# Clearing of the third V tile moved behind the first pair's row maxima; the first q and the first three weight units loaded through ScalarE's queue

## The chip, the cores and the metric

The kernel runs on one core of one Trainium2 chip. The metric is the device time of one execution in microseconds, the median of three runs. TensorE (PE) does the matrix products, VectorE (DVE), ScalarE (ACT) and GpSimd (POOL) the rest; SyncE (SP) computes nothing and starts transfers between the chip's main memory and its on-chip memory. Every engine works through its own list of instructions in order, and waits where an instruction needs a result that is not there.

## What is computed

```python
def reference(q, k, v, w_gate, w_val, w_out, w2_in, w2_out):
    # q, k, v: (2 batches, 12 heads, 448 tokens, 64), float32; weights float64
    scores = q @ k.transpose(0, 1, 3, 2) / 8
    scores = where(strictly_upper_triangle, -1e9, scores)
    attn = exp(scores - max(scores)); attn = attn / (sum(attn) + 1e-9)
    x = (attn @ v), heads side by side            # (896, 768)
    x = (sigmoid(x @ w_gate) * (x @ w_val)) @ w_out            # inner width 1536
    h = x @ w2_in                                              # inner width 2048
    return (h * clip(h + 3, 0, 6) / 6) @ w2_out                # (896, 768)
```

## The kernel before, in words

A float32 operand is carried to TensorE as two parts, `hi` and `lo = x - hi`, and each product is three matmuls (hi·hi, hi·lo, lo·hi). ACT writes the `hi` parts, DVE the `lo` parts.

**Attention** works on 12 pairs of heads. All work of a pair is cut into steps, each bound to an engine. A list scheduler (`emit_in_order`) goes through them with estimated durations and writes the instructions out in the order in which they would start by these estimates; this order is fixed when the kernel runs. In the texts a step has the pair's number in brackets:

- `Lk`, `Lq`, `Lv` (SP): load k, q, v of the pair, two transfers each (`load`, lines 208 to 227).
- `Tk`, `Tq` (PE, L247): transposes, all through one PSUM buffer `tr`, which the next transposition takes over only after `Tlk` or `Tlq`. `Thk`, `Thq` (ACT, L256): hi parts `kh`, `qh`. `Tlk`, `Tlq` (DVE, L263): lo parts `kl`, `ql`.
- `S0`, `S1`, `S2` (PE, L279 and L289): scores of query tiles 0 and 1, of tile 2, and of tile 3, with the mask added. There are two PSUM buffers for them.
- `M0` to `M3` (DVE, L300, `s_max`): row maxima of the four query tiles. `E0` to `E3` (ACT, L307, L311): exponentials and row sums. `R0` to `R3` (DVE, L316): reciprocals. `N0` to `N3` (POOL, L322): normalisation.
- `C0` to `C3` (PE, L335): transposes of the normalised rows; `H` (ACT, L345) and `J` (DVE, L351) their two parts.
- `Vh`, `Vl` (POOL, L234 and L241): the two parts of V, written into the diagonal blocks of a padded tile `vpad`. There are three such tiles, used in turn (pair p uses tile p mod 3). The off-diagonal blocks must be zero; they are cleared once, at the start, by 12 DVE memsets (L562), four for each tile. Pair 2 is the first to use the third tile.
- `D0` to `D3` (PE, L362): product with V into one buffer `pav`; `Xh` (ACT, L375) and `Xl` (DVE, L378) give it back, and `D0` of the next pair waits for `Xl`.
- 30 steps `Z` (PE, L440): products of zeros that fill the time in which TensorE would stand idle while the first pairs start.

**Weights** come in 68 units of 768 KB of 64-bit words, loaded by `load_unit` (L93, on SP) and decoded by ACT and DVE. The first three units are steps of the schedule: `W0` to `W2` (SP, the load), `Wa` (ACT, L105, scales the upper words), `Wb` (DVE, L110, shifts the lower words), `Wc` to `We` and `Wg` (DVE), `Wf` (ACT). They are decoded among the steps of the pairs, long before TensorE uses them. The order that the scheduler writes out has, on ACT, `E3(2)`, then `Thk(4)`, at the place of `W0`; `H1(2)`, then `E3(3)`, at that of `W1`; and `Wa1`, then `H0(3)`, at that of `W2`. On DVE the order from `Wb0` on is `Wb0`, `R2(3)`, `M3(3)`, `J0(2)`, `Tlq(5)`, `J1(2)`, `Wc0`, `M0(4)`, `M1(4)`, `R3(3)`, `Xl(1)`. On DVE at the start it is the memsets, `Tlk(0)`, `Tlq(0)`, `M0(0)`, `M1(0)`, `M2(0)`, `R0(0)`, `R1(0)`, `Tlq(1)`, `M3(0)`, `R2(0)`, `Tlk(1)`, `R3(0)`, `Tlq(2)`.

**Feed-forward** follows: both layers stream the weight units through TensorE, three units ahead.

Of the kernel before, what the change touches and what calls it, by code (L numbers as in the profile page):

```python
# [8 lines left out]
F32 = mybir.dt.float32  # L9
# [7 lines left out]
PSUM = bass.MemoryType.PSUM  # L17

# A float32 operand is carried to the tensor engine as two float32r parts: hi, rounded to 12
# significant bits, and lo = x - hi, which has at most 12 and so is exact.  A product is  # L20
# hi*hi + hi*lo + lo*hi; lo*lo is below half a unit of the float32 product's last place.
TERMS = ((0, 0), (0, 1), (1, 0))

# float64 weights come as raw 64-bit words.  The upper word read as float32 and scaled by 2**-112
# has the exponent of the float32 value in its low eight exponent bits, three places too far right.
REBIAS = 2.0 ** -112
# The upper word of float32's largest 12-bit value, scaled so: larger magnitudes saturate there.
UPPER_MAX = (1.0 + 0x6FFE00 / 2.0 ** 23) * 2.0 ** (31 - 127)
# [3 lines left out]
def kernel(  # L32
# [12 lines left out]
    nc = tc.nc  # L45
# [5 lines left out]
    CP = 112  # L51
    # Query tiles begin where a chunk of D keys does.
    Q0 = [0, *range(S % P or P, S, P)]
    Q1 = [*Q0[1:], S]
    NQ = len(Q0)
# [15 lines left out]

# [1 line left out]
    units = []  # L73
# [13 lines left out]

    def load_unit(u):
        if u >= NU:
            return  # L90
        src, n = units[u]
        t = wraw.tile([P, UN], U64, tag="raw", name="raw")
        nc.sync.dma_start(  # L93
            out=t.rearrange("p (a b) -> p a b", b=n),
            in_=src.rearrange("(a p) b -> p a b", p=P),
        )
        raw_t[u] = t
# [53 lines left out]
    def acc():  # L151
        """The next of four two-bank accumulators, in turn."""
        pool = psum[acc_n[0] // 2 % 2]
        acc_n[0] += 1
        return pool.tile([P, 2, 512], F32, tag="m", name="m")

    def split(hi, lo, src):
        """src (PSUM or SBUF) into its two parts."""
        nc.scalar.copy(hi, src)
        nc.vector.tensor_sub(lo, src, hi.bitcast(F32))  # L160

    def halves(ps, u, x, k0, first, last, bs=(0, 1), ks=range(6)):
        """ps[f, token] += unit u's [768, 128] block transposed times x, for batches bs."""
        w = split_t[u]
        for i in ks:
            for n, (a, c) in enumerate(TERMS):
                for b in bs:
                    nc.tensor.matmul(  # L168
                        ps[:, b, :S],
                        lhsT=w[a][:, i * P : (i + 1) * P],  # L170
                        rhs=x[c][:, k0 + i, b * S : (b + 1) * S],
                        start=(first and i == 0 and n == 0),
                        stop=(last and i == 5 and n == 2),
                    )
# [6 lines left out]
    with tc.manual_schedule():  # L181
        # ================= attention =================
        with ExitStack() as actx:
# [16 lines left out]
            NV = 3  # L200
            # V by chunks of 64 keys, the first head's over the second's, block diagonal.
            vpad = [
# [5 lines left out]
            def load(p, nm):  # L208
                b, hp = divmod(p, NPAIR)
                if nm == "v":  # L210
                    t = p_raw.tile([P, NC, D], F32, tag=nm, name=nm)
                    for j in range(2):
                        nc.sync.dma_start(
                            out=t[j * D : (j + 1) * D],
                            in_=v[b, 2 * hp + j].rearrange("(c p) d -> p c d", p=D),
                        )
                    live[nm, p] = t
                    return
                t = p_raw.tile([CP, S // CP, 2, D], F32, tag=nm, name=nm)
                for j in range(2):  # L220
                    nc.sync.dma_start(
                        out=t[:, :, j, :],
                        in_=(q if nm == "q" else k)[b, 2 * hp + j].rearrange(
                            "(c p) d -> p c d", p=CP
                        ),
                    )
                live[nm, p] = t

            def halves_of(t):
                return [t[j * D : (j + 1) * D, :, j * D : (j + 1) * D] for j in range(2)]  # L230

            def v_hi(p):
# [36 lines left out]
            def s_pe(p, ts):  # L269
                both = ps_a.tile([P, 2, 512], F32, tag="m", name="s")  # L270
                off = 0
                for t in ts:
# [13 lines left out]
                    for j in range(2):  # L286
                        # Half a tile: in the rows of the array that the head's products use.
                        r = slice(j * D, (j + 1) * D) if rows == D else slice(rows)
                        nc.tensor.matmul(  # L289
                            ps[:, j, Q0[t] :], lhsT=identb[r, r], rhs=maskb[r, r],  # L290
                            start=False, stop=True,
                        )
# [5 lines left out]
            def s_max(p, t):  # L298
                nm = column("nm", t)
                nc.vector.tensor_reduce(nm, live["s", p, t], axis=AX.X, op=ALU.max, negate=True)  # L300
                live["nm", p, t] = nm

            def s_exp(p, t):
# [22 lines left out]
            def c_pe(p, g):  # L326
                ps = ps_pt.tile([P, 512], F32, tag="pt", name="pt")
                for c, off in GROUPS[g]:
                    for t in range(NQ):
                        if Q1[t] > c * D:  # L330
                            # From the middle of a tile: its rows turned by half, and what comes
                            # after the second half is written over or not used.
                            r, rows = max(0, c * D - Q0[t]), Q1[t] - Q0[t]
                            o = off + Q0[t] + r - c * D
                            nc.tensor.transpose(  # L335
                                ps[:, o : o + rows],
                                live["pr", p, t][:, c].rearrange("p j d -> p (j d)"),
                                identf[:rows, r : r + rows],
                            )
# [39 lines left out]

            # Chunks that share a PSUM bank, with their columns there: the longest left, and the  # L380
            # longest that still fits.
            GROUPS, WIDTH, chunks = [], [], list(range(NC))
# [9 lines left out]

            # Query tiles that share a tile of scores, a bank for each head.
            STILES = [(0, 1), (2,), (3,)]

            def product(cols, stationary=P):
                """The weight of a product: its columns, or the load of its stationary operand."""
                return max(cols / 2.4 + 3, stationary / 1.2)

            # Every step of a pair: (key, engine, weight, what it follows, function).  # L400
            steps = []
# [42 lines left out]

            # While the last pairs drain: the first weights, and batch 0's part of their products.
            first_acc = []
            for u in range(3):
# [6 lines left out]

                add("W", "sp", 2000, [], load_unit)
                add("Wa", "act", 740, own("W"), dec_scale)
# [19 lines left out]

            # Buffers: how many, and (step that takes one, step that gives it back) in turn.
            def every(*uses):
# [24 lines left out]
            def emit_in_order(rank):  # L503
                """Emit the steps as a list schedule would start them: of those that can start
                first, the one of least rank."""
                left = {s[0]: s for s in steps}
# [34 lines left out]

            # How far a kind of step falls back, in pairs.
            LATE = {
# [4 lines left out]

            # The tensor engine's clock rises under load: products of zeros keep it busy while the
            # first pairs start.  # L550
            idle = const.tile([P, 512], BF16, name="idle")
# [6 lines left out]
            nc.vector.tensor_copy(maskb, maskf)  # L558
            for pair in vpad:
                for t in pair:  # L560
                    for j in range(2):
                        nc.vector.memset(  # L562
                            t[j * D : (j + 1) * D, :, (1 - j) * D : (2 - j) * D].bitcast(F32), 0.0
                        )
            emit_in_order(rank)
            for u in range(3):
                load_unit(u + 3)

        # ================= feed-forward =================
        LA = 3  # L570
# [73 lines left out]
        for c in range(2):  # L644
# [14 lines left out]
            for s in range(NS - 2):  # L659
# [7 lines left out]
                u += 1  # L667
            # The last two units go by token tile, so that the tiles are done one after another.
            advance(u)
# [43 lines left out]
```

## Time and profile before

| | |
|---|---|
| median of three runs | 624.47 us (624.44 to 624.48) |
| span of the profiled execution, first to last instruction | 620.4 us |
| time of the profiled execution itself | not recorded beside its span; the runs lie 4.07 us above the span |
| TensorE busy | 611.8 us, 99% of the span |
| VectorE, ScalarE, GpSimd busy | 413.4, 267.0, 94.3 us |

The span is what the profile can explain; the 4.07 us around it are launch and end. Busy shares are averages over stages: the attention stage ends at about 130 us, and in it ACT, DVE and POOL are nearly as busy as TensorE, while in the feed-forward stage TensorE alone sets the pace. A matmul's end is modelled, so its start is the better mark.

### The profile page before, as it was taken

The page shows a single profiled execution, that of the slowest core. Times are in us where ns is not written, and L with a number is a line of the kernel's source. Part 1 is how long each engine was busy: PE and PEld are TensorE (multiplying, and loading weights), DVE is VectorE, ACT ScalarE, POOL GpSimd, SP SyncE. Part 2 cuts the span into 40 slices and gives each one's busy share as a digit, 9 for nine tenths or more (in the row PEclk, how much of TensorE's full clock was granted, in tenths as well). Part 3 has the DMA queues.
Part 4 walks back from the last instruction along what each step waited for, and adds up shares of the span by engine and source line. Part 5 has one row for each costly group of instructions (what it writes and reads, how often), then busy time and mean ns, then how long its engine had stood idle before and what let it go on. Part 6 is the DMA issues. An engine that isn't in the chain of part 4 may idle for free.

```text
span 620.4 us, 8945 instructions
## 1 busy us (share of the span) xinstructions
PE 611.8 (99%) x3498; PEld 560.2 (90%) x3498; DVE 413.4 (67%) x604; ACT 267.0 (43%) x532; POOL 94.3 (15%) x152
## 2 busy tenths in 40 slices
PE   8999999999999999999999999999999999999997
PEld 4788788999999999999999999999999999999997
DVE  6699997556666666666655666788778888617701
ACT  3898998533333333333233222444454443223200
POOL 4889998300000000000000000000000000000000
PEclk9999999999999999999999999999999999999999
DMA  7664350013333333333333333333333345416102
GB/s 167 139 172 124 76 167 3 1 51 102 107 124 125 103 102 107 123 120 109 103 102 101 102 101 102 102 101 110 119 125 108 101 107 169 135 48 196 46 1 89
DMA packets 80489, 65.05 MB, mean 105 GB/s; under 512 B 34624, under 2 KB 76352, under 8 KB 80448
## 3 DMA queue, kind: packets, MB, share of 16 engines
q1 hardware_dynamic: 80448, 64.50, 35.0%
q8 instruction: 27, 0.44, 0.3%
q14 instruction: 14, 0.11, 0.1%
HBM read 61.73 MB, written 2.75 MB: 104 GB/s over the span
## 4 chain that ended last, share of the span: by engine, by line
PE 94%; POOL 2%; DVE 1%; ACT 1%; issue 1%; DMA 0%; SPq 0%; POOLq 0%; DVEq 0%
PE m L168 61%; PE m L651 19%; PE pav L362 5%; PE s L279 3%; PE pt L335 3%; PE s L289 1%; PE tr L247 1%; POOL pr L322 1%; DVE vpad L562 1%; POOL vpad L241 1%; ACT pr L307 0%; DMA q<-in_q_dram 0%; POOL vpad L234 0%; DVE kl L263 0%; DVE ql L263 0%
## 5 line engine op out<-in xcount | busy, mean ns | idle before, releaser
L168 PE MATMUL m<-xt,hi 128*128 128x448 f32 x576 | 142.5, 366 | 0.0
L131 ACT CAST hi<-b 128x768 fp32r<-128x768 f32 x68 | 56.9, 836 | 185.0 <-DVE b L124 162.9
L168 PEld LDWEIGHTS m<-xt,hi 128*128 128x128 f32 x576 | 107.8, 188 | 8.4
L651 PE MATMUL m<-hi,g 128*128 128x384 f32 x448 | 113.8, 334 | 0.0
L168 PE MATMUL m<-yt,hi 128*128 128x448 f32 x384 | 93.4, 365 | 0.0
L136 DVE TENSOR_TENSOR lo<-b,hi 128x768 fp32r<-128x768 f32 x68 | 64.9, 954 | 40.8 <-ACT hi L131 40.8
L168 PE MATMUL m<-xt,lo 128*128 128x448 f32 x288 | 83.8, 365 | 0.0
L651 PEld LDWEIGHTS m<-hi,g 128*128 128x128 f32 x448 | 80.8, 188 | 0.0
L168 PEld LDWEIGHTS m<-yt,hi 128*128 128x128 f32 x384 | 72.1, 188 | 5.7
L651 PE MATMUL m<-lo,g 128*128 128x384 f32 x224 | 74.8, 334 | 0.0
L168 PE MATMUL m<-g,hi 128*128 128x448 f32 x288 | 70.1, 365 | 0.0
L124 DVE SCALAR_TENSOR_TENSOR b<-raw,b 128x768 int32<-128x768 int32 x68 | 65.9, 968 | 2.3
L118 DVE SCALAR_TENSOR_TENSOR b<-b,raw 128x768 int32<-128x768 int32 x68 | 65.4, 961 | 2.3
L105 ACT ACTIVATE b<-raw 128x768 f32<-128x768 f32 x68 | 61.3, 902 | 0.0
L168 PEld LDWEIGHTS m<-xt,lo 128*128 128x128 f32 x288 | 54.1, 188 | 4.3
L168 PEld LDWEIGHTS m<-g,hi 128*128 128x128 f32 x288 | 54.1, 188 | 4.3
L168 PE MATMUL m<-yt,lo 128*128 128x448 f32 x192 | 54.5, 365 | 0.0
L322 POOL TENSOR_SCALAR pr<-pr,rc 64x64 f32<-64x64 f32 (+3 forms) x96 | 52.3, 562 | 8.7 <-DVE rc L316 7.1
L307 ACT ACTIVATE pr<-s,nm 64x64 f32<-64x64 f32 (+3 forms) x96 | 44.4, 469 | 5.9 <-PE s L289 5.2
L605 DVE TENSOR_TENSOR t<-m,t 128x896 f32<-128x896 f32 x12 | 13.1, 1091 | 47.1 <-PE m L168 47.1
L651 PEld LDWEIGHTS m<-lo,g 128*128 128x128 f32 x224 | 42.0, 188 | 0.0
L362 PE MATMUL pav<-pth,vpad 128*128 128x448 f32 (+6 forms) x168 | 41.0, 309 | 0.0
(64 smaller groups left out, 760.1 us busy)
## 6 DMA issues: line engine op xcount, KB each, us to landing
raw<-in_moe_w_out_dram SPq DMA_DIRECT2D x28, 768.0 KB, 4.4
raw<-in_moe_w_in_dram SPq DMA_DIRECT2D x16, 768.0 KB, 4.6
raw<-in_moe_w_gate_dram SPq DMA_DIRECT2D x12, 768.0 KB, 4.5
raw<-in_moe_w_val_dram SPq DMA_DIRECT2D x12, 768.0 KB, 4.3
k<-in_k_dram SPq DMA_DIRECT2D x24, 112.0 KB, 2.7
q<-in_q_dram SPq DMA_DIRECT2D x24, 112.0 KB, 3.0
v<-in_v_dram SPq DMA_DIRECT2D x24, 112.0 KB, 2.9
out_dram<-osb SPq DMA_DIRECT2D x1, 1344.0 KB, 8.5
```

Source lines behind the costliest of these rows:

```text
L105: nc.scalar.activation(b, words(u)[0].bitcast(F32), AF.Copy, scale=REBIAS)
L118: nc.vector.scalar_tensor_tensor(bi, bi, 3, words(u)[1], op0=ALU.logical_shift_left, op1=ALU.bitwise_or)
L124: nc.vector.scalar_tensor_tensor(bi, words(u)[0], -(2 ** 31), bi, op0=ALU.bitwise_and, op1=ALU.bitwise_or)
L131: nc.scalar.copy(hi, part_t[u])
L136: nc.vector.tensor_sub(lo, part_t.pop(u), split_t[u][0].bitcast(F32))
L168: nc.tensor.matmul(ps[:, b, :S], lhsT=w[a][:, i * P : (i + 1) * P], rhs=x[c][:, k0 + i, b * S : (b + 1) * S], start=(first and i == 0 and ...
L279: nc.tensor.matmul(ps[:, j], lhsT=live["q" + "hl"[a], p][r, Q0[t] : n], rhs=live["k" + "hl"[c], p][r, :n], start=(i == 0), stop=False,)
L307: nc.scalar.activation(pr[:, :, j], ps[:, j].rearrange("p (c d) -> p c d", d=D), AF.Exp, bias=nm[:, j : j + 1], accum_out=sm[:, j : j + 1],)
L322: nc.gpsimd.tensor_scalar(pr[:, :, j], pr[:, :, j], rc[:, j : j + 1], 1.0, op0=ALU.mult, op1=ALU.mult)
L335: nc.tensor.transpose(ps[:, o : o + rows], live["pr", p, t][:, c].rearrange("p j d -> p (j d)"), identf[:rows, r : r + rows],)
L362: nc.tensor.matmul(live["pav", p][:, c * D :], lhsT=vpad[p % NV][a][:, c], rhs=pt[e][:, off : off + S - c * D], start=(c == 0 and m == 0), ...
L651: nc.tensor.matmul(po[t], lhsT=g2[a][:, 2 * s + i, t * P : (t + 1) * P], rhs=w[e][:, i * HC : (i + 1) * HC], start=(s == 0 and i == 0 and ...
```

## The change

Three edits, and the removal of comments (not shown):

1. The 12 memsets at the start become 8: those for the third V tile are now issued by DVE right after the row maxima of pair 0's last query tile (`M3(0)`).
2. The two transfers of pair 0's q are issued by ACT instead of SP.
3. The loads `W0`, `W1`, `W2` are issued by ACT instead of SP. In the scheduler's estimates they remain steps of SP with the same weight, so that the order written out is the same as before.

```diff
-    def load_unit(u):
+    def load_unit(u, queue=None):
...
-        nc.sync.dma_start(
+        (queue or nc.sync).dma_start(
             out=t.rearrange("p (a b) -> p a b", b=n),
...
                 for j in range(2):
-                    nc.sync.dma_start(
+                    (nc.scalar if (nm, p) == ("q", 0) else nc.sync).dma_start(
                         out=t[:, :, j, :],
...
+            def v_zero(i):
+                for t in vpad[i]:
+                    for j in range(2):
+                        nc.vector.memset(
+                            t[j * D : (j + 1) * D, :, (1 - j) * D : (2 - j) * D].bitcast(F32), 0.0
+                        )
...
                 nc.vector.tensor_reduce(nm, live["s", p, t], axis=AX.X, op=ALU.max, negate=True)
                 live["nm", p, t] = nm
+                if (p, t) == (0, NQ - 1):
+
+                    v_zero(NV - 1)
...
-                add("W", "sp", 2000, [], load_unit)
+                add("W", "sp", 2000, [], load_unit, nc.scalar)
...
-            for pair in vpad:
-                for t in pair:
-                    for j in range(2):
-                        nc.vector.memset(
-                            t[j * D : (j + 1) * D, :, (1 - j) * D : (2 - j) * D].bitcast(F32), 0.0
-                        )
+            for i in range(NV - 1):
+                v_zero(i)
             emit_in_order(rank)
```

## Rows read from the trace of the kernel before

**Rows 1.** The page's head: the span and TensorE's busy time.
```profile
span 620.4 us, 8945 instructions
...
PE 611.8 (99%) x3498; PEld 560.2 (90%) x3498; DVE 413.4 (67%) x604; ACT 267.0 (43%) x532; POOL 94.3 (15%) x152
```

**Rows 2.** Chain of work that ended last, first 17 us: start, duration, what.
```profile
16.98 0.60 PE tr L247 x4
```

**Rows 3.** Timeline, VectorE: start, duration, line, operation, count, [idle before <- releaser].
```profile
2.11 6.62 DVE L562 MEMSET vpad<- 64x448 f32 x12
...
14.94 1.08 DVE L300 TENSOR_REDUCE nm<-s 128x2 f32<-128x896 f32 x1
...
16.30 0.62 DVE L263 SCALAR_TENSOR_TENSOR kl<-tr,kh 128x448 fp32r<-128x448 f32 x1 [0.20 <-ACT kh L256]
```

**Rows 4.** Timeline, ScalarE, the first pair's hi parts of k and q.
```profile
6.46 0.54 ACT L256 ACTIVATE kh<-tr 128x448 fp32r<-128x448 f32 x1 [4.44 <-PE tr L247]
7.71 0.54 ACT L256 ACTIVATE qh<-tr 128x448 fp32r<-128x448 f32 x1 [0.71 <-PE tr L247]
```

**Rows 5.** Timeline, TensorE, the first two pairs.
```profile
1.19 4.85 PE L440 MATMUL pt<-idle 128*128 128x512 bf16 x12 [1.19 <-DVE idle L552]
...
7.12 0.55 PE L247 MATMUL tr<-identf,q 112*128 112x112 f32 x4
7.51 1.46 PE L440 MATMUL pt<-idle 128*128 128x512 bf16 x6
...
9.97 0.24 PE L279 MATMUL s<-kh,ql 64*64 64x64 f32 x2 [0.28 <-DVE ql L263]
...
15.52 1.03 PE L440 MATMUL pt<-idle 128*128 128x512 bf16 x4
```

**Rows 6.** Timeline, SyncE's queue: issue of the first q and of W0.
```profile
1.71 1.02 SPq L221 DMA_DIRECT2D q<-in_q_dram  x2
...
28.52 0.50 SPq L93 DMA_DIRECT2D raw<-in_moe_w_gate_dram  x1
```

**Rows 7.** DMA issues, 28 to 36 us: KB each, us from issue to landing.
```profile
raw<-in_moe_w_gate_dram SPq DMA_DIRECT2D x1, 768.0 KB, 5.9
```

**Rows 8.** The same, 38 to 46 us.
```profile
raw<-in_moe_w_val_dram SPq DMA_DIRECT2D x1, 768.0 KB, 6.2
```

**Rows 9.** The same on the page, over the whole span (median).
```profile
raw<-in_moe_w_out_dram SPq DMA_DIRECT2D x28, 768.0 KB, 4.4
```

**Rows 10.** Timeline, ScalarE, around the places of W0, W1 and W2.
```profile
34.73 0.21 ACT L311 ACTIVATE sm<-sm 128x2 f32<-128x2 f32 x1
...
40.80 0.67 ACT L307 ACTIVATE pr<-s,nm 128x448 f32<-128x448 f32 x1
...
56.53 0.53 ACT L345 CAST pth<-pt 128x448 fp32r<-128x448 f32 x1 [1.44 <-PE pt L335]
```

**Rows 11.** Timeline, VectorE, from the first decoding step on.
```profile
37.72 0.54 DVE L110 TENSOR_SCALAR raw<-raw 128x768 int32<-128x768 int32 x1
38.89 0.17 DVE L316 RECIPROCAL rc<-sm 128x2 f32<-128x2 f32 x1 [0.63 <-ACT sm L311]
39.19 1.09 DVE L300 TENSOR_REDUCE nm<-s 128x2 f32<-128x896 f32 x1
...
43.25 0.59 DVE L378 TENSOR_TENSOR xt<-pav,xt 128x448 fp32r<-128x448 f32 x1
...
46.16 0.53 DVE L110 TENSOR_SCALAR raw<-raw 128x768 int32<-128x768 int32 x1
```

**Rows 12.** Timeline, TensorE: D0(2), and C0(4) with its wait.
```profile
44.09 0.45 PE L362 MATMUL pav<-pth,vpad 128*128 128x448 f32 x1
...
56.17 0.77 PE L335 MATMUL pt<-identf,pr 128*128 128x128 f32 x5 [0.27 <-POOL pr L322]
```

**Rows 13.** Timeline, GpSimd: N2(3), then Vh(4).
```profile
39.15 1.04 POOL L322 TENSOR_SCALAR pr<-pr,rc 128x320 f32<-128x320 f32 x2 [0.20 <-DMA v<-in_v_dram]
40.97 1.21 POOL L234 TENSOR_SCALAR vpad<-v 64x448 fp32r<-64x448 f32 x2 [0.78 <-PE pav L362]
```

## The prediction, made before the changed kernel was run

> **What bounds the kernel now.** I read the page first: TensorE is busy 99% of a span of 620.4 us [rows 1], so whatever delays its work in the attention stage is not made up later; in the feed-forward stage it runs without a gap. Then the chain of waits shows how the start is paced: memsets on VectorE up to 8.7 us [rows 3], the first pair's lo parts, scores and exponentials, VectorE's lo part of pair 1's k, and the transposes of pair 2's q at 16.98 us [rows 2]. From there TensorE's timeline has hardly a gap until 56.17 us, where it waits 0.27 us for GpSimd [rows 12]. So a shift of the step at 16.98 us is a shift of all that follows. Last I read the timelines of each engine, with the written-out order of the steps beside them, since an engine held at one step holds all that are behind it.
>
> **The clears, removed from the start.** 12 memsets take 6.62 us, 0.55 us each [rows 3]. With four gone, VectorE is free at 2.11 + 8 x 0.55, about 6.5 us, instead of 8.7 us. Not all 2.2 us are won. `Tlk(0)` needs ACT's hi part, done at 6.46 + 0.54 = 7.00 us, and `Tlq(0)` that of q, done at 7.71 + 0.54 = 8.25 us [rows 4]. A lo part of this shape takes 0.62 us [rows 3], so `ql` is there at about 8.9 us. TensorE is in its zero products until 7.51 + 1.46 = 8.97 us anyway [rows 5]. The third product of `S0(0)`, which started at 9.97 us when `ql` released it [rows 5], can start at 8.95 at the earliest. I take 9.02: a gain of 0.95 us. All steps behind it, up to `M3(0)` (14.94 to 16.02 us [rows 3]), wait for one another and keep that gain: `M3(0)` ends at 15.07 us.
>
> **The clears, put back.** Now 4 x 0.55 = 2.2 us of memsets stand there, until 17.28 us. Behind them are `R2(0)` (under 0.1 us) and `Tlk(1)`, which starts at 17.35 instead of 16.30 us [rows 3]. Its slack was only the wait of 0.20 us in front of it and the short reciprocal. `Tlk(1)` releases `Tq(2)` on TensorE, the step at 16.98 us [rows 2]. The clears in the new place cost 2.0 us and give 0.95 us: **+1.05 us**. I looked for cover: TensorE's zero products in front of `Tq(2)` end at 16.55 us, 15.6 us after the shift [rows 5], so nothing there hides it. GpSimd, which needs the third tile for pair 2 only, is not held; that it runs ahead gains nothing, since its next steps wait for reciprocals that come late with everything else.
>
> **The first q through ACT.** SP's issues of it take 1.02 us [rows 6], and everything behind them on SP (v of pair 0, then k, q, v of pairs 1 to 3) is issued up to 1 us earlier. Nobody waits for these: `Tq(0)` at 7.12 us has zero products right in front of it and no wait is listed [rows 5]. If ACT issues q before its first activation it lands earlier than now; if after its table load, some 0.3 us later; both are hidden behind these products. Cost and gain 0; ACT's issue time lies before its first work at 6.46 us [rows 4].
>
> **W0 through ACT.** This is the part with the largest price. On SP the load went out at 28.52 us [rows 6] and was first used by `Wb0` on VectorE at 37.72 us [rows 11]: 9.2 us for a load that took 5.9 us to land [rows 7]. On ACT its place is behind `E3(2)`, whose last instruction starts at 34.73 us [rows 10]. (All times of this paragraph are those of before; the 1.05 us shifts them together.) So 3.0 us are left for it. The row nearest above is the next unit in the same stage, 6.2 us [rows 8]; the nearest below the median over all, 4.4 us, nearly all without small loads beside them [rows 9]. I take the middle, 5.3 us, since one k pair and one v pair are in flight beside W0, fewer than in rows 7 and 8. It lands at about 40.1 us, and VectorE stands still at `Wb0` for 2.4 us. Then `Wb0` (0.46 us to the next start) and `R2(3)`, at 40.56 instead of 38.89; `M3(3)` at 40.63 instead of 39.19 us [rows 11]: +1.44 us, the rest of the stall being eaten by the wait of 0.63 us there and short gaps. From `M3(3)` to `Xl(1)` at 43.25 us VectorE has no gap, so `Xl(1)` ends at 43.84 + 1.44 = 45.28 us [rows 11]. `D0(2)` on TensorE needs it and started at 44.09 us [rows 12]; it moves to 45.33: +1.24 us. At 56.17 us TensorE gets 0.27 us back from its wait for GpSimd [rows 12], if GpSimd is not late too. GpSimd starts `N2(3)` 0.26 us after `R2(3)`, so at 40.82, ends it 1.04 us later, and `Vh(4)` comes at 41.86 instead of 40.97 us, +0.89, behind which GpSimd works through [rows 13]. The larger, 1.24 - 0.27 = **+0.97 us**, holds. The bounds: landing after 4.4 us gives `M3(3)` +0.54 and `D0(2)` +0.34, at 56.17 us +0.1 us; after 6.2 us, +2.34, +2.14, and +1.9 us.
>
> Here a rule is weighed. The rows show two loads of this stage at 5.9 and 6.2 us on SP's ring, and with ACT's queue W0 would no longer stand behind q and k in that ring [rows 7, 8]. The Trainium skill (DMA: Bandwidth & Descriptors, "Issuing engines are not separate DMA queues") says that transfers started by any engine run on the same 16 DMA engines and interleave, so that a second issuer saves issue time alone. By that rule W0 stays near 5.9 us, and the sum would be 1.6 us for this part; were ACT's queue a way of its own, 4.4 us and 0.1 us. No run here has yet shown ACT's queue.
>
> **W1, W2 and ACT's issue time.** W1 goes out before `E3(3)`, at 40.80 us [rows 10], and is used by `Wb1` at 46.16 us [rows 11]: 5.4 us, just enough at 5.3 us, 0.8 us late at 6.2 us. W2 has more room. Each issue holds its queue 0.50 us [rows 6]; W0's lies inside the stall above, the other two can delay ACT by 1.0 us in a stretch where it has no gap until its wait of 1.44 us at 56.53 us [rows 10], which is the cover. Bounds 0 and 1.8 us; I take **+0.3 us**, nearer the lower end because the steps in between have slack on both sides. SP is freed of three issues of 0.5 us; its loads wait for buffers, not for SP: 0.
>
> **The sum.** 1.05 + 0.97 + 0.3 = +2.3 us on the span of 620.4 us [rows 1]. The runs lie 4.07 us above that span, and nothing of the change lies outside it: 624.47 + 2.3 = **626.8 us**. From no change this measurement can tell about 0.2%, 1.25 us.
>
> **The rivals.**
> - *W0 is in time after all, not slower.* If VectorE is not held at `Wb0` (landing within about 4.4 us, or ACT's queue taking the load while `E3(2)` still computes), only the clears remain: 624.47 + 1.05 = 625.5 us, within 0.2%. For it: 4.4 us is the commonest landing [rows 9]. Against: both rows of this stage are 1.5 us above [rows 7, 8], and the instruction in front of W0 waits for the one before it. It decides below 4.4 us. Chance 0.18.
> - *The clears cost nothing in the new place either.* Were `Tlk(1)` not what paces TensorE at 16.98 us, 0.95 us would be won: with W0 in time 623.5 us, and less only if GpSimd's lead also shortened its later waits. Against it the chain, which runs through exactly this step [rows 2, 3]. Chance 0.12; 0.07 of it below the 0.2% line.
> - *All three loads late, and ACT's issue time felt in full:* W0 after 6.2 us (+1.9) and 1.8 us for the rest: 1.05 + 1.9 + 1.8, 629.2 us. Chance 0.10.
> - *The clock falls.* TensorE is left without work from 15.6 us to `Tq(2)` at 18.0 us; before, the waits of this kind that the rows show are 0.28 and 0.27 us [rows 5, 12]. Its first 12 zero products took 4.85 us, 0.40 each, the later six 1.46 us, 0.24 each [rows 5]: the lower level of 1.2 GHz at first, then 2.4 GHz. If it fell back for as long as it took at first (some 5 us), about 2.5 us would be lost more: 629.3 us. Chance 0.04. The Trainium skill (TensorE: Matmul & The Clock Gate, "HAM oscillation") tells of such falls in idle gaps; no row here shows one.
>
> **How the numbers follow.** The forecast (clears, and W0 late) has 0.56. Its own range is 1.05 + 0.1 to 1.05 + 1.9 + 0.3, 625.6 to 627.7 us. To leave out no more than 2 in 10, the range goes down to 625.2, which takes in W0 in time, and up to 628.8 us. Slower by over 0.2%: 0.56 + 0.10 + 0.04, all but nothing of the forecast below the line, 0.70; within 0.2%: 0.18 + 0.05 = 0.23; faster 0.07.
>
> **What would show it.** In the changed profile: `S0(0)` done about 0.95 us earlier; four memsets between `M3(0)` and `R2(0)`; `Tq(2)` at about 18.0 us; W0 issued at about 35.9 us, 1 us behind its place above; VectorE waiting for that load 1.5 to 3.2 us at L110; `D0(2)` at 46.4 us; the feed-forward stage the same, only later. The prediction is wrong if `Tq(2)` is not later than 16.98 us, or if L110 does not wait.

## The result, and the profile after

The changed kernel takes 629.52 us in the median of 5 runs (626.65 to 632.11); runs of the kernel before beside them have a median of 624.44 us (622.17 to 624.48). The ratio is 1.0096, 95% interval 1.0066 to 1.0125: slower by about 1%. The forecast was 626.8 us in a range of 625.2 to 628.8 us: the direction is right, the size is not, and the median lies above the range.

The profiled execution took 628.09 us, its span 626.3 us, so only 1.8 us lie outside the span. The span of before is 620.4 us [rows 1]: its profiled execution was one of those at 622.2 us, not at 624.47 us. So the change cost 5.9 us from span to span. This execution is not the median one. The spans of the five runs are 624.8, 626.3, 627.7, 627.8 and 630.3 us, and TensorE's mean granted clock falls in the same order, 0.997, 0.992, 0.991, 0.988 and 0.986 of full speed. So what the others have more or less goes with the clock; where in them it fell is not on record. Here is TensorE's timeline in the profile after (start, duration, line, operation, count, and in brackets the idle time in front and what ended it); it answers to [rows 5, 12].

```profile
7.56 1.46 PE L450 MATMUL pt<-idle 128*128 128x512 bf16 x6
...
9.09 0.22 PE L286 MATMUL s<-kh,ql 64*64 64x64 f32 x2
...
14.62 1.03 PE L450 MATMUL pt<-idle 128*128 128x512 bf16 x4
18.05 0.60 PE L254 MATMUL tr<-identf,q 112*128 112x112 f32 x4 [2.40 <-DVE kl L270]
...
46.43 1.94 PE L345 MATMUL pt<-identf,pr 128*128 128x128 f32 x8 [1.25 <-DVE ptl L361]
...
50.17 0.45 PE L372 MATMUL pav<-pth,vpad 128*128 128x448 f32 x1
```

The third product of `S0(0)` starts at 9.09 instead of 9.97 us, 0.88 us earlier. `Tq(2)` starts at 18.05 instead of 16.98 us [rows 2], after a wait of 2.40 us; before, the wait in front of it was 0.43 us. `D0(2)` is at 50.17 instead of 44.09 us [rows 12], 6.1 us late, so the loss arises between 15 and 50 us. VectorE's timeline of the same kernel, which answers to [rows 3, 11], shows the two places where it is held:

```profile
14.04 1.08 DVE L307 TENSOR_REDUCE nm<-s 128x2 f32<-128x896 f32 x1
15.15 2.12 DVE L235 MEMSET vpad<- 64x448 f32 x4
17.30 0.17 DVE L326 RECIPROCAL rc<-sm 128x2 f32<-128x2 f32 x1
17.39 0.60 DVE L270 SCALAR_TENSOR_TENSOR kl<-tr,kh 128x448 fp32r<-128x448 f32 x1
...
44.13 0.56 DVE L110 TENSOR_SCALAR raw<-raw 128x768 int32<-128x768 int32 x1 [2.91 <-DMA raw<-in_moe_w_gate_dram]
44.61 0.16 DVE L326 RECIPROCAL rc<-sm 128x2 f32<-128x2 f32 x1
44.68 1.07 DVE L307 TENSOR_REDUCE nm<-s 128x2 f32<-128x896 f32 x1
...
47.33 1.37 DVE L114 TENSOR_SCALAR b<-b 128x768 f32<-128x768 f32 x1
...
49.36 0.59 DVE L388 TENSOR_TENSOR xt<-pav,xt 128x448 fp32r<-128x448 f32 x1
```

The four memsets stand between `M3(0)` and `R2(0)`, and `Tlk(1)` starts at 17.39 instead of 16.30 us. At 44.13 us `Wb0` has waited 2.91 us for W0. The issue of W0, now in ScalarE's timeline, answers to [rows 6, 10], and its landing (DMA issues from 37 to 39 us: KB each, us to landing) to [rows 7]:

```profile
37.75 0.20 ACT L321 ACTIVATE sm<-sm 128x2 f32<-128x2 f32 x1
37.76 0.45 ACTq L93 DMA_DIRECT2D raw<-in_moe_w_gate_dram  x1
```

```profile
raw<-in_moe_w_gate_dram ACTq DMA_DIRECT2D x1, 768.0 KB, 6.4
```

What I had given a chance of 0.04 is in the table by stretches: stretch in us, busy us of PE, PEld, DVE, ACT, POOL with instruction counts, TensorE's granted clock as a part of full speed, DMA share, GB/s. The first row is before, the others are after.

```profile
20.00:25.00 5.00, 4.70 (x35) 3.26 (x35) 3.73 (x9) 4.90 (x19) 4.66 (x8) 1.00 0.54 120
```

```profile
15.00:20.00 5.00, 2.60 (x23) 1.54 (x21) 3.23 (x9) 2.34 (x7) 4.67 (x9) 0.92 0.67 152
20.00:25.00 5.00, 5.00 (x26) 3.82 (x26) 3.06 (x8) 3.52 (x14) 4.57 (x8) 0.50 0.25 58
25.00:30.00 5.00, 5.00 (x46) 4.02 (x44) 4.25 (x9) 4.25 (x14) 1.04 (x2) 0.90 0.37 83
...
46.00:50.00 4.00, 3.57 (x18) 2.94 (x18) 4.00 (x9) 3.58 (x12) 3.66 (x5) 0.57 0.57 191
```

Behind the 2.40 us of idle time TensorE runs at the lower level (0.50, that is 1.2 GHz) from about 19 to 26 us; before, all these stretches show 1.00. It falls once more at 46 us, behind the waits that W0 causes.

**Where the 5.9 us go.** `Tq(2)` is 1.07 us late. `S0(2)` starts at 27.90 us against 24.90 us in the timeline of before, 3.00 us late: 1.93 us more, the clock's part: from `Tq(2)` to `S0(2)` it is 9.85 us here against 7.92 us before, and 7.91 us again in two kernels below in which this wait is filled and the clock stays at 1.00. `C0(4)`, behind its wait for GpSimd, is at 62.06 against 56.17 us [rows 12], 5.89 us late: 2.89 us from W0. From there to the end the distance stays the same: 1.07 + 1.93 + 2.89 = 5.89 us.

### The profile page after: what moved, and what is told of

Its sections match the earlier page's. It is cut to its first block, busy times and chain, and to the rows that moved or that the text cites. A ratio compares the mean times of both kernels' runs of the same rounds, so it can differ in the third digit from the quotient of the medians.

```text
span 626.3 us, 8945 instructions
## 1 busy us (share of the span) xinstructions
PE 615.5 (98%) x3498; PEld 563.2 (90%) x3498; DVE 414.4 (66%) x604; ACT 268.1 (43%) x532; POOL 94.2 (15%) x152
## 4 chain that ended last, share of the span: by engine, by line
PE 92%; POOL 3%; DVE 2%; DMA 1%; issue 1%; ACT 1%; SPq 0%; DVEq 0%; POOLq 0%
PE m L168 61%; PE m L657 19%; PE pav L372 4%; PE s L286 3%; PE pt L345 3%; POOL pr L332 1%; PE pt L450 1%; PE s L296 1%; PE tr L254 1%; DMA raw<-in_moe_w_gate_dram 1%; POOL vpad L248 1%; ACT pr L317 0%; DVE nm L307 0%; DMA q<-in_q_dram 0%; POOL vpad L241 0%
```

## The experiments

All are timed against the kernel before on the same chip. A diff is against the changed kernel where nothing else is said. The kernel before doesn't have one time: in the 35 runs of the second group it lies at 622.2 (14 runs within 0.2 us), at 622.9 to 623.9, or at 624.5 to 624.8 us (10 runs). So the table gives the lowest time too, which compares executions with the fewest such extras.

| kernel | lowest | median | highest | ratio, 95% interval |
|---|---|---|---|---|
| before (27, 35 and 16 runs beside the experiments) | 622.19 | 622.48, 622.92, 622.70 | 624.78 | |
| changed kernel | 626.65 | 629.52 | 632.11 | 1.0096 (1.0066 to 1.0125) |
| clears_only | 624.63 | 625.07 | 626.22 | 1.0035 (1.0022 to 1.0049) |
| queues_only | 624.86 | 625.54 | 627.54 | 1.0044 (1.0028 to 1.0060) |
| q_only | 622.24 | 624.54 | 624.66 | 1.0009 (0.9994 to 1.0023) |
| clears_fill | 623.87 | 624.46 | 625.38 | 1.0023 (1.0012 to 1.0035) |
| clears_pool | 620.55 | 621.18 | 623.34 | 0.9967 (0.9953 to 0.9980) |
| early_w | 622.57 | 622.72 | 625.66 | 1.0004 (0.9989 to 1.0018) |
| w12_act | 622.18 | 622.91 | 624.54 | 0.9999 (0.9985 to 1.0013) |
| fill75 | 622.19 | 622.30 | 623.08 | 0.9985 (0.9975 to 0.9996) |
| after_fill | 624.53 | 626.43 | 627.34 | 1.0045 (1.0027 to 1.0063) |
| best | 620.58 | 621.02 | 622.05 | 0.9970 (0.9960 to 0.9980) |

**clears_only**: of the change, only the clears; q and W0 to W2 stay on SP.

```diff
-                    (nc.scalar if (nm, p) == ("q", 0) else nc.sync).dma_start(
+                    nc.sync.dma_start(
...
-                add("W", "sp", 2000, [], load_unit, nc.scalar)
+                add("W", "sp", 2000, [], load_unit)
```

> Only the clears of the third V tile move behind the first pair's maxima; all loads stay on SyncE's queue. Theory: the new place costs 1.07 us at the transposes of pair 2's q (start 18.05 instead of 16.98 us), and the wait of 2.4 us in front of them lets TensorE's clock fall, which costs about 2 us more between 19 and 26 us: +3.0 us, ratio 1.005, and W0 is not waited for. Rival A, the wait does not cause the fall (it comes from elsewhere in the changed kernel): +1.05 us, ratio 1.0017, clock 1.00 in 15 to 30 us. Rival B, the loss comes from the queues alone: no change.

Measured +2.4 us at the lowest, ratio 1.0035; the mean granted clock is 0.994 or 0.995 in all eight runs. The wait in front of `Tq(2)` is 2.40 us again, and the granted clock from 15 us on:

```profile
15.00:20.00 5.00, 2.60 (x24) 1.71 (x22) 2.89 (x8) 1.97 (x6) 4.76 (x8) 0.85 0.81 184
20.00:25.00 5.00, 5.00 (x26) 3.83 (x26) 3.24 (x8) 3.70 (x14) 4.22 (x7) 0.50 0.33 73
```

`Tq(2)` starts at 17.68 us, 0.70 us late, because in this execution the first 12 zero products took 4.53 us, where they took 4.91 us in the changed kernel's; `S0(2)` starts at 27.51 us, 2.61 us late. So the clock costs 1.91 us here as well. Rival A (the fall comes from elsewhere) and rival B (the queues alone) do not hold.

**clears_fill**: as clears_only, and TensorE's wait filled; the diff is against clears_only.

```diff
             def t_pe(p, nm):
+                if (p, nm) == (2, "q"):
+                    for _ in range(11):
+                        z_pe(0)
```

> The clears moved as in the first of these, all loads on SyncE's queue, and 11 further products of zeros on TensorE in front of pair 2's transposes of q, which fill the 2.4 us in which TensorE would wait there. Theory: the idle stretch is what lets the clock fall; with it filled the clock stays at 1.00 and only the place of the clears is paid: +1.05 us, ratio 1.0017. Rival, the clock falls for another reason: as without the filling, about +3 us.

Measured +1.7 us at the lowest, more than the 1.05 us expected. `Tq(2)` starts without a wait, in TensorE's timeline, and the clock holds in the same stretches:

```profile
18.25 0.60 PE L257 MATMUL tr<-identf,q 112*128 112x112 f32 x4
```

```profile
15.00:20.00 5.00, 4.97 (x37) 2.60 (x35) 3.34 (x9) 2.52 (x7) 4.70 (x8) 1.00 0.74 167
20.00:25.00 5.00, 4.48 (x37) 3.20 (x37) 3.62 (x10) 4.04 (x16) 4.66 (x9) 1.00 0.51 116
```

`S0(2)` starts at 26.16 us: 1.26 us late instead of 2.61 or 3.00 us. Of this, 0.2 us come from the start of this execution, whose first 12 zero products took 5.10 us (4.91 us in the changed kernel's). Filling idle time with useless work wins 1.35 us at this point against clears_only; that the idle stretch makes the clock fall is shown, and no run of the 12 has a mean clock below 0.997. In the times only 0.6 us (median) to 0.8 us (lowest) of it are left: most of these runs lose some of the clock elsewhere, the profiled one behind the wait at 75 us that fill75 below is about. The Trainium skill (TensorE: Matmul & The Clock Gate, "HAM oscillation — how this bites in real kernels") says that waits between groups of matmuls throw TensorE back to its slow clock; these rows agree with it, 0.50 without the filling and 1.00 with it. The waits in its example are longer than the 2.40 us that were enough here.

**queues_only**: of the change, only the loads; all 12 clears at the start.

```diff
-                if (p, t) == (0, NQ - 1):
-                    v_zero(NV - 1)
...
-            for i in range(NV - 1):
+            for i in range(NV):
                 v_zero(i)
```

> Only the loads move: the first q and the first three weight units through ScalarE's queue; all 12 clears stay at the start. Theory: VectorE waits at the first decoding step (L110) some 2.9 us for W0, and TensorE loses about 2.9 us behind it, the clock stays at 1.00: +2.9 us, ratio 1.0046. Rival, the lateness matters only because the clears had already shifted the steps against each other: under +1.5 us, ratio below 1.0024.

Measured +2.6 us at the lowest, ratio 1.0044. `Tq(2)` is at 17.00 us, as before. W0 landed after 5.1 us here, and VectorE's and GpSimd's timelines show what follows:

```profile
39.94 0.56 DVE L110 TENSOR_SCALAR raw<-raw 128x768 int32<-128x768 int32 x1 [1.69 <-DMA raw<-in_moe_w_gate_dram]
...
40.49 1.07 DVE L307 TENSOR_REDUCE nm<-s 128x2 f32<-128x896 f32 x1
...
43.14 1.39 DVE L114 TENSOR_SCALAR b<-b 128x768 f32<-128x768 f32 x1
...
45.18 0.59 DVE L385 TENSOR_TENSOR xt<-pav,xt 128x448 fp32r<-128x448 f32 x1
```

```profile
42.97 2.54 POOL L248 TENSOR_TENSOR vpad<-v,vpad 64x448 fp32r<-64x448 f32 x2
```

`M3(3)` comes 1.30 us late (40.49 against 39.19 us [rows 11]), as the prediction's working gives for a landing after 5.1 us. But `Xl(1)` comes 1.93 us late, because `Wc0` (L114) behind it took 1.39 us, and in the kernel before never more than 0.73 us, which it took at this place:

```profile
41.86 0.73 DVE L114 TENSOR_SCALAR b<-b 128x768 f32<-128x768 f32 x1
```

`C0(4)` starts at 58.03 instead of 56.17 us: W0 costs 1.86 us here. The rest of the 3.4 us of this execution's span (623.8 us) is a fall of the clock at 76 us (0.79 in the mean of 74 to 82 us). Another run, with a mean clock of 1.000, has a span of 623.1 us, so in it the loads cost 2.7 us without any fall: what W0 costs differs between executions.

**q_only**: only the first q on ACT's queue. Against the kernel before, the edit is the one line `(nc.scalar if (nm, p) == ("q", 0) else nc.sync).dma_start(` of the change.

> Only the first q goes through ScalarE's queue. Theory: nobody waits for it, 0.0 us, ratio 1.000; SyncE issues the next loads 1 us earlier and the transposes of the first q start at the same 7.1 us. Rival, the earlier loads help or the earlier traffic holds the first k back: the transposes of the first k start elsewhere than at 5.9 us and the time moves by up to 1 us.

Lowest 622.24 us against 622.22 us of before beside it: 0. The transposes of the first k do start elsewhere, as the rival has it, at 5.58 instead of 5.87 us, but behind zero products that were done earlier (12 in 4.55 us instead of 4.85 us). The ratio's interval includes 1. The median lies high because 6 of these 10 runs, and 6 of the 27 of before beside them, lie at 624.5 us or above, with mean clocks of 0.994 or 0.995. The profiled one (624.66 us) shows two falls of the clock, one of 0.79 from 74 to 82 us and one of 0.67 from 10 to 15 us:

```profile
10.00:15.00 5.00, 5.00 (x32) 3.14 (x34) 2.48 (x6) 2.95 (x14) 1.70 (x4) 0.67 0.85 191
```

The earlier one made TensorE 0.95 us late, as `C0(6)` behind the wait at 75 us shows (76.00 against 75.05 us); the later one makes up the other 1.55 us of its span (622.9 us). Whether loading q this way makes such executions more frequent stays open.

**w12_act**: W1 and W2 on ACT's queue, W0 and q on SP; the diff is against the kernel before.

```diff
-                add("W", "sp", 2000, [], load_unit)
+                add("W", "sp", 2000, [], load_unit, nc.scalar if u else nc.sync)
```

> Only W1 and W2 go through ScalarE's queue, at the places that they have in the changed kernel; W0 and the first q stay on SyncE's. Theory: W0 alone makes the loss of queues_only; here 0 to +0.3 us. Rival, ScalarE's issue time and the second load's lateness are part of it: +0.7 us or more.

Lowest 622.18 us, ratio 0.9999, span 620.4 us as before: 0. At these places ACT's issue time and the later two loads cost nothing. With q at 0 too, W0 alone makes the loss of queues_only.

**early_w**: as queues_only, with the three loads issued earlier on ACT's queue.

```diff
             def t_hi(p, nm):
+                if nm == "q" and 3 <= p < 6:
+                    load_unit(p - 3, nc.scalar)
...
-                add("W", "sp", 2000, [], load_unit, nc.scalar)
+                add("W", "sp", 2000, [], lambda u: None)
```

> As queues_only (first q and W0 to W2 through ScalarE's queue, clears at the start), but each of the three loads is issued earlier on that queue: in front of the hi parts of q of pairs 3, 4 and 5 (24, 31 and 40 us). Theory: it was the late place and not the queue that cost; W0 then has some 13 us to land, VectorE doesn't wait for it, and the time is that of before within 0.3 us. Rival, the second ring itself or ScalarE's issue time costs: still +1 us or more with no wait for W0.

Lowest 622.57 us, +0.4 us, ratio 1.0004; span 620.8 us, and VectorE doesn't wait for W0. The queue is not what cost, the late place on it is. The 0.4 us that are left begin at W0's issue, in ScalarE's timeline:

```profile
24.01 0.39 ACTq L93 DMA_DIRECT2D raw<-in_moe_w_gate_dram  x1
24.45 0.54 ACT L265 ACTIVATE qh<-tr 128x448 fp32r<-128x448 f32 x1 [0.24 <-issue]
```

Before, this hi part started at 24.10 us. TensorE's transposes at 28.06 us come at 28.42 us, and `C0(4)` at 56.54 instead of 56.17 us. So the rival holds to this extent: where ACT has no slack, the time that it spends on an issue is lost.

**fill75**: the kernel before, with zero products in TensorE's wait for GpSimd at 75 us; they write into columns that the transposes behind them write over; the diff is against the kernel before.

```diff
+                            if (p, g, t) == (6, 0, NQ - 1):
+                                for _ in range(16):
+                                    nc.tensor.matmul(
+                                        ps[:, Q0[t] :], lhsT=idle[:, :P], rhs=idle[:, : 512 - Q0[t]],
+                                        start=True, stop=True,
+                                    )
```

> The kernel before, and 16 products of zeros on TensorE within the transposes of pair 6 (C0), where it waits 1.4 us for GpSimd at 75 us. They fill part of that wait and their results are written over. Theory: the two levels of the kernel before (622.2 and 624.5 us) are executions in which TensorE's clock did not fall and did fall after that wait; with it filled the upper level is seen seldom or not at all, and the lowest time stays 622.2 us. Rival, the levels come from elsewhere: the same two levels as before.

No run of 11 lies above 623.1 us, where 16 of 35 runs of the kernel before beside it do, 10 of them at 624.5 to 624.8 us. This is the wait, in TensorE's timeline of before:

```profile
75.05 0.33 PE L335 MATMUL pt<-identf,pr 128*128 128x128 f32 x1 [1.43 <-POOL pr L322]
```

So a fall of the clock behind this wait is part of the upper level, at which also the three times lie that stand ahead of the prediction. It is not all of it: the runs of before have mean clocks of 0.999 or 1.000 at 622.2 to 622.4 us, 0.997 at 622.9 to 623.9 us, and 0.994 or 0.995 at 624.5 to 624.8 us. That suggests none, one and two falls; q_only's profile, at the upper level, shows two, of which the one at 75 us cost 1.55 us. The run of fill75 at 623.08 us, with 0.997, still has one. In the stretch from 74 to 82 us the first row is fill75, the second queues_only:

```profile
74.00:82.00 8.00, 7.88 (x77) 6.47 (x75) 6.93 (x14) 6.33 (x22) 6.50 (x10) 1.00 0.13 29
```

```profile
74.00:82.00 8.00, 6.56 (x45) 5.30 (x43) 5.71 (x11) 4.82 (x15) 5.21 (x8) 0.79 0.14 33
```

**after_fill**: the changed kernel in full, with the 11 zero products of clears_fill.

> The changed kernel in full, and the 11 products of zeros in front of pair 2's transposes of q. Theory: the loss of the changed kernel is the sum of three parts: the place of the clears (1.1 to 1.3 us), the clock's fall in the wait there (about 2 us, now gone), and W0's lateness (1.9 to 2.9 us). So the lowest time is that of before plus 3.2 to 4.2 us, 625.4 to 626.4 us, about 1 to 2 us below the changed kernel in the median (629.5); the clock is 1.00 from 15 to 30 us, and may still fall behind the wait for W0. Rival, the parts don't add up: as the changed kernel, or as clears_fill.

Median 626.43 us, 3.1 us below the changed kernel; lowest 624.53 us, lower than I expected, the next 626.06 us. The clock is 1.00 from 15 to 52 us. `S0(2)` is 0.60 us late, `C0(4)` (59.73 us) 3.56 us: W0 costs 2.96 us, with the load landing after 6.3 us, late enough to hold VectorE for 2.83 us. Three runs with a mean clock of 1.000 have spans of 624.1 to 624.7 us, 3.7 to 4.3 us above before, so the parts add up about as expected. W0 costs as much here as in the changed kernel (2.89 us), so the fall at 46 us there added nothing that these profiles show: at full clock TensorE waits 0.85 us for `Xl(1)` in front of `D0(2)`.

**clears_pool**: as clears_only, but the third tile is cleared by GpSimd at the start; the diff is against clears_only.

```diff
-            def v_zero(i):
+            def v_zero(i, engine=nc.vector):
...
-                        nc.vector.memset(
+                        engine.memset(
...
-                if (p, t) == (0, NQ - 1):
-                    v_zero(NV - 1)
...
             for i in range(NV - 1):
                 v_zero(i)
+            v_zero(NV - 1, nc.gpsimd)
```

> The clears of the third V tile leave VectorE's start but go to GpSimd, right after the masks, where it has nothing to do until V of the first pair lands at 5.8 us; all loads stay on SyncE's queue. Theory: the gain of the start (0.95 us at the first scores) is real and is kept when the clears stand on no path: -0.95 us, ratio 0.9985, the transposes of pair 2's q at about 16.0 us, clock 1.00 in 10 to 30 us. Rival, the gain at the start is eaten by the next wait: 0.0 us.

Faster: ratio 0.9967, lowest 620.55 us, 1.64 us below before, where 0.95 us was expected. GpSimd clears in a stretch in which it only waited:

```profile
1.76 1.97 POOL L235 MEMSET vpad<- 64x448 f32 x4
5.50 1.23 POOL L241 TENSOR_SCALAR vpad<-v 64x448 fp32r<-64x448 f32 x2 [1.77 <-DMA v<-in_v_dram]
```

`Tq(2)` starts at 16.44 us in the profiled execution, 0.54 us earlier than before. With VectorE out of the way the start is paced by the zero products, whose first 12 took 5.26 us here and 4.24 us in the profile of the next kernel. With the 4.85 us of before, `Tq(2)` would be at about 16.03 us, an estimate from these numbers, and that is what was expected. Before, the memsets set the start: with 12 of them in front `Tq(2)` was at 16.98 us whether the first products took 4.79 us (w12_act) or 5.30 us (early_w). So an execution in which the zero products are done early gains more than 0.95 us here.

**best**: clears_pool and fill75 together.

> clears_pool and fill75 together: the clears of the third V tile on GpSimd at the start, all loads on SyncE's queue, products of zeros in pair 6's wait at 75 us. Theory: the lowest time is that of clears_pool, 620.6 us, and the executions at 623.3 us are no longer seen: median about 621.0 us, ratio 0.997 or below. Rival, the wait at 75 us is a different one now and the filling delays it: median as clears_pool's or above, 621.2 us.

Median 621.02 us, ratio 0.9970 (0.9960 to 0.9980), and no run above 622.1 us, where 3 of the 12 of clears_pool lie at 623.3 us: some 1.7 us faster than the kernel before, and 8.5 us below the changed one's median. TensorE's start in its profile:

```profile
1.18 4.24 PE L453 MATMUL pt<-idle 128*128 128x512 bf16 x12 [1.18 <-DVE idle L565]
...
15.41 0.60 PE L254 MATMUL tr<-identf,q 112*128 112x112 f32 x4 [0.43 <-DVE kl L270]
```

## Why the prediction was right or wrong

- **The place of the clears.** Predicted +1.05 us and `Tq(2)` at 18.0 us; measured 1.07 us and 18.05 us. The mechanism is right, with the gain of the start a little smaller (0.88 for 0.95 us) and the memsets shorter (2.12 us). That the size came out to 0.02 us is luck: the gain goes by the zero products of one execution, and in the four profiled kernels with the clears in this place `Tq(2)` started between 17.59 and 18.25 us, 0.61 to 1.27 us late.
- **The clock.** This is the step that failed: "The clock falls. TensorE is left without work from 15.6 us to `Tq(2)` at 18.0 us … Chance 0.04". The forecast left this cost out of its sum. The place and the price (2.5 us) were there; it fell in both profiles with this idle stretch and cost 1.93 and 1.91 us. The reason given for the low chance was that no row of before shows a fall. Those rows are of one execution, and other executions of the same kernel do lose time to a fall (fill75). The working set a wait of 2.4 us beside waits of 0.28 and 0.27 us; the longest of its kind in the same profile was 1.43 us, at 75 us. One reading in it stays unconfirmed: the first zero products took 0.40 us each, but the granted clock of these stretches reads 1.00 in the profile.
- **W0.** This failed by as much. The mechanism was right: late landing, `Wb0` stops VectorE, `Xl(1)` and `D0(2)` follow. The term was mis-sized: +0.97 us within 0.1 to 1.9 us; measured 1.86 us (queues_only), 2.89 us (changed kernel) and 2.96 us (after_fill). Three things make up the 1.92 us of the changed kernel. The load took 6.4 us there (5.1 us in queues_only), where I took 5.3 us between 4.4 and 6.2 us. I had counted one k pair and one v pair in flight beside it; SP's timeline in the profile after has transfers of q as well, four issues from 40.23 to 44.29 us. `Wc0`, shifted into GpSimd's subtractions for V, took 1.37 us for at most 0.73 us. And the 0.27 us that I subtracted for the wait at 56.17 us did not come: in queues_only, where this can be read, `C0(4)` still waits 0.29 us for GpSimd, which is late by as much. Why W0 landed in 5.1 us in one profile and in 6.4 us in another with the same loads beside it stays open.
- **The two together.** The spans differ by 5.9 us where the sum gave 2.3 us. Of the 3.6 us between, the clock is 1.93 us and W0 1.92 us, less the 0.3 us for W1 and W2 that did not come.
- **The rule weighed there.** On ACT's queue W0 took 5.1 and 6.4 us, where such loads took 5.9 and 6.2 us on SP's [rows 7, 8]. The sentence of the Trainium skill (DMA: Bandwidth & Descriptors, "Issuing engines are not separate DMA queues") agrees with that: the second queue gave no clearly faster transfer, and what it saved in issue time on SP nobody waited for. It is not a test of the rule, since other loads stood beside W0 in each case.
- **q, W1, W2.** Predicted 0 for q, measured 0. Predicted 0.3 us for W1, W2 and ACT's issues; measured 0 (w12_act), though an issue of ACT's cost 0.36 us at another place (early_w).
- **The base of the sum.** "The runs lie 4.07 us above that span, and nothing of the change lies outside it" was wrong. Only 1.8 us lie outside. The other 2.3 us are falls of the clock that the three runs shown had and the profiled execution had not: one is behind the wait at 75 us (fill75), and q_only's profile points to a second, at 10 to 15 us. Adding terms of one execution to a median of others hid that.

## What to carry to other kernels

Work moved off the start of an engine has to land where that engine, and the one that waits for it next, have slack: behind the maxima VectorE had a wait of 0.20 us for 2.12 us of memsets, on GpSimd the same clears were free. A wait of TensorE has two prices: its length, and the clock that may fall behind it; when a change opens an idle stretch in TensorE, such as the 2.4 us here, count both, test with filler products, and look for the next wait behind which the clock may fall instead. A load that moves to a queue of a computing engine goes out when that engine reaches it, so compare its new place, not its queue, with its first use; the issue itself takes time on that engine.

## What was not expected of the hardware

- A granted clock of 1.00 in one profile doesn't mean that other executions have it: the kernel before has runs at 622.2 and at 624.5 us, and with 16 small filler products in one wait of 1.4 us none of 11 runs lies above 623.1 us.
- A VectorE operation on 128x768 float32 (L114) takes 0.55 us in the median, and 1.39 us while GpSimd works on V through the whole of it (43.14 to 44.53 us within 42.97 to 45.51 us). In before, where GpSimd's subtraction began at 42.26 us, the same step from 41.86 us on took 0.73 us. That sharing of something between the two engines is the cause was only argued.
- The first 12 zero products take between 4.24 us (best) and 5.30 us (early_w) in these profiles of one and the same start. The granted clock reads 1.00 there in before, so the rows don't show why.
